# Cosine attention and a mixture-of-experts MLP on one core: from scheduled groups to an order written out by hand

## Chip, core and metric

One core of a Trainium2 chip runs the whole program in one launch. The metric is the device time of one execution in microseconds (us); lower is better. The runs listed are 674.89, 676.12 and 678.36 us, median 676.12.

## What is computed

Inputs are q, k and v of shape (8 batches, 12 heads, 448 tokens, 64), all float32, and tau = 0.1.

```python
q_n = q / (norm(q) + 1e-6);  k_n = k / (norm(k) + 1e-6)       # over the 64
attn = softmax(q_n @ k_n.T / tau)                              # per batch and head
x = (attn @ v).transpose(0, 2, 1, 3).reshape(3584, 768)
h = x @ w_in                                                   # 768 x 2048
out = (h * sigmoid(1.702 * h)) @ w_out                         # 2048 x 768
```

## The kernel before

Heads are handled in 48 pairs, so that two heads of 64 fill 128 partitions, and pairs in 16 groups of three; two groups make a batch. Tokens are cut in four chunks of 112.

The six row blocks of w_in and the sixteen of w_out are loaded as float32 through one staging buffer (`wst`) and cast to fp16 on ScalarE (line 93) and VectorE (line 99).

`emit_front` loads q, k and v of a group by SyncE (lines 111 and 117), squares on ScalarE (line 124), sums on VectorE (line 126) and finds 1/norm of the whole group on VectorE by a reciprocal, a polynomial and two Newton steps (lines 133 to 147). `emit_back` goes pair by pair: GpSimd scales q and k to fp16 (line 163), puts ones beside v and casts v (lines 170, 171); TensorE transposes (line 176, tile `tpsum`), VectorE copies the result to `qkT` (line 182); TensorE forms the scores of a chunk for both heads, each on 64 rows of the array (line 188, `spsum`), ScalarE takes Exp (line 196); per head four matmuls accumulate values and, in row 65, the softmax's denominator (line 209, `avps`), evicted by VectorE (line 217). Denominators go through DRAM (lines 218, 226), one reciprocal on six partitions (line 229), back to DRAM and out as one broadcast per head (line 234); VectorE multiplies (line 238), and a DMA puts the product into `xT` (line 241).

`emit_moe` takes a batch of 448 tokens: sixteen groups of six matmuls (line 254, `hps`), Tanh on ScalarE (line 262), one VectorE operation that makes `gT` (line 263); then for each of four 112-token tiles and two column halves sixteen matmuls (line 276, `ops`), a copy on ScalarE (line 283) and one store per tile (line 289). The halves of x * sigmoid are folded: tanh(0.851 h) + 1, and 0.5 in the last copy.

The order between engines is left to the scheduler of the tile framework, which takes instructions by priority in the order of the program: front of a group, back of the group before, MoE when a batch is complete. PSUM has two buffers for scores (`ps_sp`) and one each for transposes, `avps`, `hps` and `ops`.

## Time and profile before

| what | value |
|---|---|
| median of three runs | 676.12 us (674.89 to 678.36) |
| profiled execution | span 674.3 us from first to last instruction; no other time is listed for it |
| TensorE, VectorE, ScalarE, GpSimd busy | 529.9, 344.0, 338.5, 134.6 us |
| DMA | 68.49 MB, all issued by SyncE |

The profile is of one execution. Busy time of TensorE counts matmuls, whose ends are modelled and which overlap, so it is more than the work needs back to back. PE is TensorE, PEld its weight loads, DVE VectorE, ACT ScalarE, POOL GpSimd, SP SyncE. Idle time before an instruction is put down to what released it.

### The profile page before, as it was taken

Reading aid. Unit: us, or ns where it says so; the run is one execution under the profiler, and the core shown is the slowest. Engines: PE = TensorE matmul, PEld = TensorE weight load, DVE = VectorE, ACT = ScalarE, POOL = GpSimd, SP = SyncE. Lnnn points to the kernel's source line nnn. Section 1 sums busy time; section 2 is a strip of 40 time slices with the busy share of each in tenths; the row PEclk is TensorE's granted clock in tenths of the full one; section 3 lists DMA queues with packets and bytes.
Section 4 is the critical chain, followed back from the end, with each engine's and each line's share of the span. In section 5 each row is a group of like instructions: output and inputs, shape, how many; then the busy total and the mean of one; then the engine's idle time right before and its main releaser. Section 6 shows DMA issues by size and latency. Waiting matters only on the chain. (4 is left out here: it accounts for less than half of the span.)

```text
span 674.3 us, 8804 instructions
## 1 busy us (share of the span) xinstructions
PE 529.9 (79%) x2944; PEld 294.0 (44%) x2944; DVE 344.0 (51%) x640; ACT 338.5 (50%) x439; POOL 134.6 (20%) x199
## 2 busy tenths in 40 slices
PE   0095518578998889989988889899999998786566
PEld 0032203134564446544644455446544653453244
DVE  0336535567847784468266734674296136312210
ACT  4383507267737763667347735764476345212211
POOL 1214022034124323032123211240233000000000
PEclk9999855599999999999999999999999999999999
DMA  8875655545564446134424441344321211030002
GB/s 209 233 183 130 183 153 141 138 90 119 131 166 108 103 112 157 56 82 108 134 61 103 109 120 54 92 117 124 83 56 39 73 41 42 23 81 20 1 20 62
DMA packets 156878, 68.49 MB, mean 102 GB/s; under 512 B 137856, under 2 KB 150432, under 8 KB 156064
## 3 DMA queue, kind: packets, MB, share of 16 engines
q1 hardware_dynamic: 156832, 67.93, 40.1%
q8 instruction: 23, 0.38, 0.2%
q14 instruction: 23, 0.19, 0.1%
HBM read 51.20 MB, written 11.18 MB: 93 GB/s over the span
## 5 line engine op out<-in xcount | busy, mean ns | idle before, releaser
L254 PE MATMUL hps<-xT,w_in 128*128 128x448 f16 x768 | 173.1, 355 | 54.3 <-DVE gT L263 38.5
L196 ACT ACTIVATE expT<-spsum,negbias 112x896 f16<-112x896 f32 x192 | 185.4, 1007 | 50.7 <-PE spsum L188 43.8
L276 PE MATMUL ops<-w_out,gT 128*112 128x384 f16 x1024 | 196.7, 327 | 11.5 <-ACT ost L283 7.4
L276 PEld LDWEIGHTS <-gT 128*112 128x112 f16 x1024 | 131.9, 130 | 65.1 <-issue 20.0
L263 DVE SCALAR_TENSOR_TENSOR gT<-th,hps 128x448 f16<-128x448 f16 x128 | 78.0, 610 | 134.7 <-ACT th L262 134.4
L254 PEld LDWEIGHTS <-w_in 128*128 128x128 f16 x768 | 73.7, 98 | 130.3 <-issue 61.4
L163 POOL TENSOR_TENSOR qks<-qk,ry 112x512 f16<-112x512 f32 x96 | 99.5, 1063 | 134.6 <-PE tpsum L176 74.1
L262 ACT ACTIVATE th<-hps 128x448 f16<-128x448 f32 x128 | 69.6, 544 | 111.4 <-PE hps L254 108.0
L209 PE MATMUL avps<-expT,v 112*65 112x448 f16 x384 | 111.7, 385 | 10.8 <-DVE av_sb L217 7.7
L283 ACT ACTIVATE ost<-ops 112x384 f32<-112x384 f32 x64 | 31.5, 492 | 122.2 <-PE ops L276 117.7
L188 PE MATMUL spsum<-qkT 64*112 64x448 f16 x384 | 78.2, 415 | 11.5 <-ACT expT L196 8.5
L126 DVE TENSOR_REDUCE n<-sq 112x16 f16<-112x1024 f16 x48 | 58.1, 1212 | 52.0 <-ACT sq L124 52.0
L217 DVE CAST av_sb<-avps 65x448 f16<-65x448 f32 x96 | 58.9, 613 | 38.6 <-PE avps L209 37.9
L176 PE MATMUL tpsum<-ident,qks 112*128 112x112 f16 x384 | 35.0, 229 | 52.2 <-POOL qks L163 52.2
L124 ACT ACTIVATE sq<-qk 112x1024 f16<-112x1024 f32 x48 | 50.6, 1054 | 29.9 <-DMA qk<-in_k_dram 26.9
L238 DVE TENSOR_TENSOR rcpb<-av_sb,rcpb 64x448 f16<-64x448 f16 x96 | 42.2, 457 | 45.0 <-DMA rcpb<-rcp_dram 44.1
L209 PEld LDWEIGHTS <-v 112*65 112x65 f16 x384 | 42.6, 117 | 49.3 <-issue 33.2
L176 PEld LDWEIGHTS <-qks 112*128 112x128 f16 x384 | 25.5, 106 | 70.4 <-POOL qks L163 57.2
L170 POOL MEMSET v<- 112x8 f16 x48 | 6.6, 142 | 233.3 <-PE avps L209 228.3
L188 PEld LDWEIGHTS <-qkT 64*112 64x112 f16 x384 | 25.2, 132 | 60.7 <-issue 52.2
L229 DVE RECIPROCAL rcg<-dnm 6x448 f16<-6x448 f16 x16 | 46.9, 2933 | 0.4 <-DMA dnm<-den_dram 0.4
L171 POOL CAST v<-v 112x512 f16<-112x512 f32 x48 | 29.6, 616 | 47.9 <-DMA v<-in_v_dram 47.9
(19 smaller groups left out, 94.4 us busy)
## 6 DMA issues: line engine op xcount, KB each, us to landing
qk<-in_q_dram SPq DMA_DIRECT2D x96, 112.0 KB
qk<-in_k_dram SPq DMA_DIRECT2D x96, 112.0 KB
v<-in_v_dram SPq DMA_DIRECT2D x96, 112.0 KB
out_dram<-ost SPq DMA_DIRECT2D x32, 336.0 KB
wst<-in_moe_w_in_dram SPq DMA_DIRECT2D x6, 1024.0 KB
wst<-in_moe_w_out_dram SPq DMA_DIRECT2D x16, 384.0 KB
rcpb<-rcp_dram SPq DMA_DIRECT2D x96, 56.0 KB
xT<-rcpb SPq DMA_DIRECT2D x96, 56.0 KB
```

The costliest lines, as they stand in the source:

```text
L124: nc.scalar.activation(out=sq, in_=qk32, func=AF.Square)
L126: nc.vector.tensor_reduce(out=n2[:, gi], in_=sq, axis=AX.X, op=ALU.add)
L163: nc.gpsimd.tensor_tensor(out=qks[:, ti], in0=qk32[:, ti], in1=rs_all[:, gi, ti, :, :, None].to_broadcast((P, NCH, 2, D)), op=ALU.mult,)
L176: nc.tensor.transpose(out=tpsum[:, ti, c * P : (c + 1) * P], in_=qks[:, ti, c], identity=ident[:P, :P],)
L188: nc.tensor.matmul(out=spsum[:, j, :S], lhsT=qkT[64 * j : 64 * (j + 1), 1, c * P : (c + 1) * P], rhs=qkT[64 * j : 64 * (j + 1), 0, :], sta ...
L196: nc.scalar.activation(out=expT, in_=spsum[:, :, :S], func=AF.Exp, bias=negbias[:P], scale=inv_tau,)
L209: nc.tensor.matmul(out=avps, lhsT=v65[:, c, j, :], rhs=expTs[c][:, j, :], start=(c == 0), stop=(c == NCH - 1),)
L217: nc.vector.tensor_copy(out=av_sb, in_=avps)
L254: nc.tensor.matmul(out=hps, lhsT=w_in_sb[kk][:, 128 * m : 128 * (m + 1)], rhs=xT_sb[kk][:, tok0 : tok0 + S], start=(kk == 0), stop=(kk == ...
L262: nc.scalar.activation(out=th, in_=hps, func=AF.Tanh, scale=0.851)
L263: nc.vector.scalar_tensor_tensor(out=gT[:, m, :], in0=th, scalar=1.0, in1=hps, op0=ALU.add, op1=ALU.mult,)
L276: nc.tensor.matmul(out=ops, lhsT=gT[:, kk, P * mt : P * (mt + 1)], rhs=w_out_sb[kk][:, NW * n : NW * (n + 1)], start=(kk == 0), stop=(kk = ...
```

## The change

Every engine's queue now holds its instructions in the order in which the program writes them (`manual_schedule`). The program is a loop over steps; step s treats half of pair s // 2. A table `later` says in which step each other piece of work stands: loads of q and k six pairs ahead and of v five, squares three pairs ahead, scaling two pairs ahead, transposes one, the attend of the pair before. The second half of attention's output rows is made directly on partitions 64 to 127: four standing tiles `vt` hold 128 columns for each head: v, a column of ones, and zeros. So the normalised product is written to `xT` in place and no DMA moves it.

When the six pairs of a batch are normalised, `queue_moe` puts its matmuls into a list, and `fill` takes from that list three times in each step, until a nominal 1.04 to 1.07 us are spent. Batches go in twos for the second matmul, with seven tiles of 128 tokens for two batches (three tiles with the first, four with the second), so that a tile's rows go out in two stores. MoE matmuls share three PSUM buffers; transposes and attend share one.

Norms are square roots by pow on GpSimd, one per pair, then an addition and a reciprocal on VectorE. Denominators of a group come in on 112 partitions, and their reciprocals go out as two broadcasts. Weights are loaded by eight DMAs on GpSimd's queue that cast to fp16: w_in in steps -1, 1, 3 and 5, w_out in steps 9, 11, 13 and 15. Squares are kept in float32. The last batch is queued in step 101 and runs with nothing beside it.

The core of the diff; of what it takes out, the listing above has nearly all:

```diff
-RS_C2 = -0.031518428176595475
-RS_C1 = 0.5141912670046448
-RS_C0 = 0.5009886404507127
+MM1_NS = 189
+MM2_NS = 163
+STEP_NS = 3150
+AV_SCALE = 2.0**-11
...
+    p_in = pool("p_in", 6)
+    p_v = pool("p_v", 4)
+    p_sq = pool("p_sq", 3)
+    p_n = pool("p_n", 4)
+    p_qks = pool("p_qks", 3)
+    p_qkT = pool("p_qkT", 2)
+    p_exp = pool("p_exp", 8)
+    p_av = pool("p_av", 6)
+    p_rc = pool("p_rc", 2)
+    p_x = pool("p_x", 2)
+    p_g = pool("p_g", 1)
+    p_th = pool("p_th", 3)
+    p_o = pool("p_o", 3)
...
+    ps_s = psum("ps_s", 2)
+    ps_a = psum("ps_a", 1)
+    ps_m = psum("ps_m", 3)
+    ctx.enter_context(tc.manual_schedule())
...
+    def load_qk(x):
+        b, h0 = x // HP, (x % HP) * 2
+        for d, src, nm in ((q32, q, "q32"), (k32, k, "k32")):
+            d[x] = p_in.tile([P, 2, C, D], FP32, name=nm)
             nc.sync.dma_start(
+                out=d[x].rearrange("p h c d -> p h (c d)"),
+                in_=src[b, h0 : h0 + 2].rearrange("h (p c) d -> p h (c d)", p=P),
             )
...
+    def norm(x):
+        nrm = p_n.tile([P, 2, 2, C], FP32, name="nrm")
+        nc.gpsimd.tensor_tensor(
+            out=nrm,
+            in0=n2s.pop(x),
+            in1=half_c[:P, :, None, None].to_broadcast((P, 2, 2, C)),
+            op=ALU.pow,
+        )
+        nc.vector.tensor_scalar(
+            out=nrm, in0=nrm, scalar1=1e-6, scalar2=None, op0=ALU.add
+        )
+        rss[x] = p_n.tile([P, 2, 2, C], FP32, name="rs")
+        nc.vector.reciprocal(out=rss[x], in_=nrm)
...
+    def cast_v(x):
+        src = v32.pop(x)
+        vt = vts[x % 4]
+        for j in range(2):
+            nc.gpsimd.tensor_copy(out=vt[:, :, j, 64 * j : 64 * j + D], in_=src[:, j])
+    def transposes(x):
+        tps = ps_a.tile([128, 2, S], FP16, name="tps", tag="a")
+        qks = qkss.pop(x)
+        for ti in (1, 0):
+            for c in range(C):
+                nc.tensor.transpose(
+                    out=tps[:, ti, c * P : (c + 1) * P],
+                    in_=qks[:, ti, c].rearrange("p j d -> p (j d)"),
+                    identity=ident[:P, :P],
+                )
+        qkTs[x] = p_qkT.tile([128, 2, S], FP16, name="qkT")
+        nc.vector.tensor_copy(out=qkTs[x], in_=tps)
...
+    def attend(x, j):
+        if j == 0:
+            avs[x] = p_av.tile([128, 2, S], FP16, name="av")
+        ps = ps_a.tile([128, S], FP32, name="avp", tag="a")
+        for c in range(C):
+            nc.tensor.matmul(
+                out=ps,
+                lhsT=vts[x % 4][:, c, j],
+                rhs=exps[x, c][:, j],
+                start=(c == 0),
+                stop=(c == C - 1),
+            )
+        n = D + 1 if j == 0 else 128
         nc.vector.tensor_scalar(
+            out=avs[x][:n, j], in0=ps[:n], scalar1=AV_SCALE, scalar2=None, op0=ALU.mult
+        )
...
+    def den_rcp(g):
+        r = p_rc.tile([P, 2 * GRP * S // P], FP16, name="rcg")
+        with nc.allow_low_precision("fp16 reciprocal of softmax denom"):
+            nc.vector.reciprocal(out=r, in_=dnms.pop(g))
+        rcps[g] = dram.tile([2 * GRP, S], FP16, name="rcp")
+        nc.sync.dma_start(out=flat(rcps[g]), in_=r)
+        rcbs[g] = p_rc.tile([128, GRP, S], FP16, name="rcb")
+        for j in range(2):
+            nc.sync.dma_start(
+                out=rcbs[g][64 * j : 64 * (j + 1)],
+                in_=rcps[g]
+                .rearrange("(i j) s -> j i s", j=2)[j][None]
+                .to_broadcast((64, GRP, S)),
             )
...
+    def mm1_stream(b):
+        if b % 2 == 0:
+            gts[b // 2] = p_g.tile([128, KT2, 2 * S], FP16, name="gT")
+        gT = gts[b // 2][:, :, (b % 2) * S : (b % 2 + 1) * S]
         for m in range(KT2):
+            ps = ps_m.tile([128, 512], FP32, name="mm", tag="mm")
             for kk in range(KT1):
                 nc.tensor.matmul(
+                    out=ps[:, :S],
+                    lhsT=w_in_sb[:, kk, 128 * m : 128 * (m + 1)],
+                    rhs=xTs[b, kk],
                     start=(kk == 0),
                     stop=(kk == KT1 - 1),
                 )
+                if kk == KT1 - 1:
+                    th = p_th.tile([128, S], FP16, name="th")
+                    nc.scalar.activation(out=th, in_=ps[:, :S], func=AF.Tanh, scale=0.851)
+                    nc.vector.scalar_tensor_tensor(
+                        out=gT[:, m],
+                        in0=th,
+                        scalar=1.0,
+                        in1=ps[:, :S],
+                        op0=ALU.add,
+                        op1=ALU.mult,
+                    )
+                yield MM1_NS
...
+    def store(b2, t, ost, cols):
+        i0, i1 = 128 * t, 128 * (t + 1)
+        while i0 < i1:
+            n = min(i1, (i0 // P + 1) * P) - i0
+            b, c, p0 = 2 * b2 + i0 // S, (i0 % S) // P, i0 % P
+            rows = out[b * S : (b + 1) * S].rearrange("(p c) m -> c p m", c=C)[c]
+            nc.sync.dma_start(
+                out=rows[p0 : p0 + n, cols],
+                in_=ost[i0 - 128 * t : i0 - 128 * t + n, cols],
             )
+            i0 += n
+    def mm2_stream(b2, tiles, last):
...
+        for t in tiles:
+            ost = p_o.tile([128, DM], FP32, name="ost")
+            for n in range(2):
+                cols = slice(NW * n, NW * (n + 1))
+                ps = ps_m.tile([128, 512], FP32, name="mm", tag="mm")
                 for kk in range(KT2):
                     nc.tensor.matmul(
+                        out=ps[:, :NW],
+                        lhsT=gT[:, kk, 128 * t : 128 * (t + 1)],
+                        rhs=w_out_sb[:, kk, cols],
                         start=(kk == 0),
                         stop=(kk == KT2 - 1),
                     )
+                    if kk == KT2 - 1:
+                        nc.scalar.activation(
+                            out=ost[:, cols], in_=ps[:, :NW], func=AF.Copy, scale=0.5
+                        )
+                        if last and t == tiles[-1]:
+                            store(b2, t, ost, cols)
+                        elif n == 1:
+                            store(b2, t, ost, slice(0, DM))
+                    yield MM2_NS
+    streams = []
+    def fill(ns):
+        while ns > 0 and streams:
+            try:
+                ns -= next(streams[0])
+            except StopIteration:
+                streams.pop(0)
+    def queue_moe(b):
+        streams.append(mm1_stream(b))
+        tiles = (0, 1, 2) if b % 2 == 0 else (3, 4, 5, 6)
+        streams.append(mm2_stream(b // 2, tiles, b == B - 1))
+    def load_w_in(i):
+        n = slice(512 * i, 512 * (i + 1))
+        nc.gpsimd.dma_start(
+            out=w_in_sb[:, :, n], in_=moe_w_in.rearrange("(k p) n -> p k n", p=128)[:, :, n]
+        )
+    def load_w_out(i):
+        n = slice(4 * i, 4 * (i + 1))
+        nc.gpsimd.dma_start(
+            out=w_out_sb[:, n], in_=moe_w_out.rearrange("(k p) n -> p k n", p=128)[:, n]
+        )
+    for x in range(NPAIR):
+        at(2 * (x - 6), load_qk, x)
+        at(2 * (x - 5), load_v, x)
+        for ti in range(2):
+            at(2 * (x - 3) + ti, square, x, ti)
+            at(2 * (x - 3) + ti + 1, reduce, x, ti)
+        at(2 * (x - 2), norm, x)
+        at(2 * (x - 2) + 1, scale, x, 1)
+        at(2 * (x - 2) + 1, scale, x, 0)
+        at(2 * (x - 2) + 1, cast_v, x)
+        for j in range(2):
+            at(2 * (x + 1) + j, den_out, x, j)
+        if x % GRP == GRP - 1:
+            s = 2 * (x + 1) + 1
+            d = 2 if x < HP else 1
+            at(s, den_in, x // GRP)
+            at(s + d, den_rcp, x // GRP)
+            for i in range(GRP):
+                at(s + 2 * d + 1 + i // 2, normalise, x - GRP + 1 + i)
+        if x % HP == HP - 1:
+            at(2 * (x + 1) + 1 + 2 * d + 2, queue_moe, x // HP)
+    for i in range(4):
+        at(-1 + 2 * i, load_w_in, i)
+        at(9 + 2 * i, load_w_out, i)
...
+    for s in range(min(later), max(max(later), 2 * NPAIR + 2) + 1):
+        x, half = s // 2, s % 2
+        jobs = later.pop(s, [])
+        if 0 <= x < NPAIR:
+            scores(x, half)
+            exp(x, 2 * half)
+        fill(STEP_NS * 0.33)
+        if 0 <= x < NPAIR:
+            exp(x, 2 * half + 1)
+        if 0 <= x - 1 < NPAIR:
+            attend(x - 1, half)
+        for f, a in jobs[: len(jobs) // 2]:
+            f(*a)
+        fill(STEP_NS * 0.33)
+        if half == 1 and 0 <= x + 1 < NPAIR:
+            transposes(x + 1)
+        for f, a in jobs[len(jobs) // 2 :]:
+            f(*a)
+        fill(STEP_NS * 0.34)
+    fill(1e9)
```

## Rows read from the trace of the kernel before

**Rows 1.** Windows: stretch, length, PE, PEld, DVE, ACT, POOL busy, PEclk, DMA share, GB/s.

```profile
0.00:135.00 135.00, 62.18 (x236) 24.30 (x237) 59.63 (x117) 60.26 (x58) 28.67 (x49) 0.81 0.66 171
135.00:573.00 438.00, 398.14 (x2337) 226.11 (x2337) 265.62 (x495) 258.30 (x344) 105.94 (x150) 1.00 0.39 96
573.00:674.30 101.30, 69.57 (x372) 43.59 (x370) 18.73 (x30) 19.92 (x38) 0.00 (x0) 1.00 0.12 35
```

**Rows 2.** TensorE's timeline, 300 to 318 us: start, duration, instructions.

```profile
308.17 0.35 PE L209 MATMUL avps<-expT,v 112*65 112x448 f16 x1 [0.32 <-ACT expT L196]
...
310.08 0.92 PE L209 MATMUL avps<-expT,v 112*65 112x448 f16 x4
310.94 0.40 PE L188 MATMUL spsum<-qkT 64*112 64x448 f16 x2
311.37 1.29 PE L254 MATMUL hps<-xT,w_in 128*128 128x448 f16 x6
...
312.76 0.59 PE L188 MATMUL spsum<-qkT 64*112 64x448 f16 x4
313.27 0.57 PE L176 MATMUL tpsum<-ident,qks 112*128 112x112 f16 x8
```

**Rows 3.** Timeline of the end stretch, 640 to 652 us.

```profile
643.71 1.29 PE L254 MATMUL hps<-xT,w_in 128*128 128x448 f16 x6 [1.13 <-DVE gT L263]
...
647.24 2.76 PE L276 MATMUL ops<-w_out,gT 128*112 128x384 f16 x16 [0.58 <-ACT ost L283]
```

**Rows 4.** Groups by line and shape, ScalarE: busy us, mean ns | idle before, releasers.

```profile
L196 ACT ACTIVATE expT<-spsum,negbias 112x896 f16<-112x896 f32 x192 | 185.4, 1007 | 50.7 <-PE spsum L188 43.8 <-PE avps L209 4.5
...
L262 ACT ACTIVATE th<-hps 128x448 f16<-128x448 f32 x128 | 69.6, 544 | 111.4 <-PE hps L254 108.0 <-DVE rt L142 2.0 <-DVE ry L147 0.7
...
L124 ACT ACTIVATE sq<-qk 112x1024 f16<-112x1024 f32 x48 | 50.6, 1054 | 29.9 <-DMA qk<-in_k_dram 26.9 <-DVE ry L138 1.6 <-DMA v<-in_v_dram 0.7
```

**Rows 5.** Groups by line and shape, VectorE.

```profile
L263 DVE SCALAR_TENSOR_TENSOR gT<-th,hps 128x448 f16<-128x448 f16 x128 | 78.0, 610 | 134.7 <-ACT th L262 134.4
...
L217 DVE CAST av_sb<-avps 65x448 f16<-65x448 f32 x96 | 58.9, 613 | 38.6 <-PE avps L209 37.9
L126 DVE TENSOR_REDUCE n<-sq 112x16 f16<-112x1024 f16 x48 | 58.1, 1212 | 52.0 <-ACT sq L124 52.0
...
L229 DVE RECIPROCAL rcg<-dnm 6x448 f16<-6x448 f16 x16 | 46.9, 2933 | 0.4 <-DMA dnm<-den_dram 0.4
...
L182 DVE COPY qkT<-tpsum 128x896 f16<-128x896 f16 x48 | 29.2, 607 | 16.0 <-PE tpsum L176 15.8
```

**Rows 6.** Line 238, the normalising product: duration ns min/median/max, first and last start.

```profile
L238 DVE TENSOR_TENSOR rcpb<-av_sb,rcpb x96: 320/382/1224, 71.9 to 599.6; 64x448 f16<-64x448 f16 x96
```

**Rows 7.** Groups by line and shape, GpSimd.

```profile
L163 POOL TENSOR_TENSOR qks<-qk,ry 112x512 f16<-112x512 f32 x96 | 99.5, 1063 | 134.6 <-PE tpsum L176 74.1 <-DVE ry L147 43.4 <-issue 7.3
...
L171 POOL CAST v<-v 112x512 f16<-112x512 f32 x48 | 29.6, 616 | 47.9 <-DMA v<-in_v_dram 47.9
...
L170 POOL MEMSET v<- 112x8 f16 x48 | 6.6, 142 | 233.3 <-PE avps L209 228.3 <-DMA xT<-rcpb 5.0
```

**Rows 8.** Tile v, SyncE's issues of its loads: duration ns min/median/max.

```profile
L117 SPq DMA_DIRECT2D v<-in_v_dram x96: 312/462/2307, 3.3 to 512.0; - x96
```

**Rows 9.** Windows, 25 to 30 us.

```profile
25.00:30.00 5.00, 0.00 (x0) 0.00 (x0) 3.26 (x13) 1.60 (x1) 1.03 (x2) 1.00 1.07 298
```

**Rows 10.** Windows, 101 to 119 us.

```profile
101.00:119.00 18.00, 15.71 (x58) 6.40 (x59) 10.82 (x17) 12.93 (x14) 3.81 (x6) 0.50 0.50 134
```

**Rows 11.** TensorE's timeline, 50 to 135 us.

```profile
115.92 1.70 PE L209 MATMUL avps<-expT,v 112*65 112x448 f16 x4
```

**Rows 12.** The chain that ended last: start us, duration us, what.

```profile
431.09 2.54 DMA rcpb<-rcp_dram
...
511.69 1.66 DMA den_dram<-av_sb
```

**Rows 13.** Timeline of the last 10 us.

```profile
670.17 0.49 ACT L283 ACTIVATE ost<-ops 112x384 f32<-112x384 f32 x1 [2.85 <-PE ops L276]
```

320 lines of the change are left out of this document (100 added, 220 removed).

## The prediction

> **What bounds the kernel now.** I read the engines in three stretches first, since the page's slices fill up late and thin out early [rows 1]: TensorE is the busiest in each, 62.2 us of the first 135, 398.1 of the next 438, 69.6 of the last 101.3, and its granted clock is 0.81 on average in the first, 1.00 after. So some 73 us are idle before the pipeline runs, 40 inside it and 32 behind it.
>
> Next is what the matrix work needs back to back. One matmul alone shows about 0.35 us, of which some 0.17 is drain, so a group of n costs its shown time less 0.17 [rows 2, 3]: hps (1.29 - 0.17) / 6 = 0.188 us; ops (2.76 - 0.17) / 16 = 0.162; avps 0.188; a pair of spsum matmuls, which run side by side, 0.59 - 0.40 = 0.19; a transpose (0.57 - 0.17) / 8 = 0.05. A pair of heads therefore needs 8 x 0.188 + 4 x 0.19 + 8 x 0.05 = 2.66 us, the 48 pairs 128, the 768 hps matmuls 144 and the 1,024 ops matmuls 166: 438 of the 674.3 us. The other 236 are gaps and half clock. In the end stretch the gap can be seen in one line [rows 3]: each hps group starts 1.13 us late, held by VectorE's gT, since hps has one PSUM buffer.
>
> **The change, part by part.** The order is now written out: a step is half a pair (two score blocks, two Exp, one head's attend), and in each step three fills of MoE matmuls. A fill runs until 1.04 us or more are spent: six hps matmuls (1.13 us) or seven ops matmuls (1.13 us). A filled step thus holds 1.33 us of attention and 3.4 of MoE, 4.73 us of TensorE.
>
> *Output tiles of 128 tokens.* 28 tiles x 2 x 16 = 896 ops matmuls instead of 1,024: 128 x 0.162 = 20.7 us less on the bound engine. TensorE's need falls to 418 us.
>
> *Other engines in a filled step.* ScalarE: two Exp 2.01, a Square of half the elements (bounds 0.53, half of the row, and 1.05; I take 0.6, as a short operation keeps its fixed part), three Tanh 1.63 in an hps step: 4.25 us [rows 4]. VectorE: three gT 1.83, an eviction 0.61, half a qkT copy 0.3, half a reduction 0.6, one normalising product 0.38, small norm work 0.2: 3.9 us [rows 5, 6]. Both lie beside TensorE's 4.73, with little to spare. If that cover goes, each 0.1 us of excess per step costs 7 us, as there are 71 filled steps. Both queues are in order: behind a Tanh that waits for its hps group stands the second Exp, behind gT the eviction of avps, and for that waits the transposition of the next pair, since avps and transposes now share one PSUM buffer. Behind the normalisation stands the qkT copy, for which the next scores wait; that is the stall that I expect to be late next. I take 4% (0.2 us a step) for such seams; the bounds are 0 and the 9% that TensorE idles in the present middle (40 of 438) [rows 1].
>
> *GpSimd.* Per pair two scalings 2.1 and two casts of v, some 0.7, with pow added [rows 7]. No row shows pow; it has 16 elements per partition. Below stands the 0.14 of a memset, above the 1.06 of a 512-element product; I take 0.3, as the element count is near the memset's. It is 3.1 us of a pair's 9.9: covered. The Newton steps leave VectorE, 16 times a dozen operations, which were not on the path.
>
> *Weights cast by DMA.* The 22 staging loads, 6 casts on ScalarE and 16 on VectorE go; 8 loads on GpSimd's queue come. No DMA goes out from GpSimd in this trace. The nearest row is SyncE issuing a v load of 448 pieces: 0.46 us in the middle of its cases, 2.3 at the longest [rows 8]. A quarter of w_in has 768 pieces, so I bound the issue by 0.46 and by 2.3 x 768 / 448 = 4.0 and take 2 us, since software on GpSimd is nearer to its scaling, 2 ns an element, 1.6 us for 768. It is hidden: in the early stage a pair takes 6.8 us, of which GpSimd needs 3.1, so 3.7 are free, and one such load stands behind the scalings of each pair. The Trainium skill, "SBUF — State Buffer", section "SBUF: two separate sides", speaks against this edit: descriptors of a GpSimd DMA can't be written while a VectorE instruction that takes both ports runs. That the two engines do hold each other up, this trace shows: the product of two SBUF tensors takes 0.32 us at least and up to 1.22, about one GpSimd scaling more [rows 6].
>
> *SyncE's queue.* 144 input loads for 288, 32 broadcasts of the reciprocal for 96, none of the 96 xT copies, and 58 output stores for 32 (each tile crosses one border of 112 tokens). Its pieces grow from 256 B to 1 KB. den_in waits on SP for den_out to land, and behind it stand loads that are needed three pairs later: nothing.
>
> **The sum.** *Start.* ScalarE's order puts the squares of three pairs ahead of the first Exp. 1.8 MB at 298 GB/s [rows 9] take 6 us and land 2.5 later; reduction, pow, two scalings, transposes and copy run beside the later squares: 12 us (10 to 16).
>
> *Steps 0 to 18*, attention alone: ScalarE needs 2.6 us a step. But TensorE is then likely at 1.2 GHz: in 101 to 119 us, attention with little else, the granted clock was 0.50 and four avps took 1.70 us, against 0.92 later [rows 2, 10, 11]. 58 matmuls in those 18 us are 2.4 pairs, 3.7 us per half pair. By step 19, 13 pairs of q, k, v and the weights have moved, 21.5 MB; at 298 GB/s that is 72 us from the beginning, which allows 3.2 us a step. Between 2.6 and 3.7 I take 3.4, nearest to the cold row: 65 us. The Trainium skill, "DMA: Bandwidth & Descriptors", section "Specifications", gives about 358 GB/s for a core; by that the same bytes need 60 us, DMA drops out, and the sum would be some 4 us lower. No window here reaches it.
>
> *Steps 19 to 95.* A batch's MoE fills 9.9 steps (even) or 11.4 (odd) out of 12, so 70.7 steps are filled: 70.7 x 4.93 = 349 us. The other 6.3 have only attention: 2.9 us each, 18.
>
> *Steps 96 to 101.* The rest of batch 6 (11 us) runs beside the last pair's chain: attend some 6 us in, then eviction 0.6, three short hops through DRAM at 1.7, the reciprocal 0.3 (24 elements a partition, where 448 take 2.93) [rows 5], the broadcast 2.5, six products 2.3 [rows 6, 12]: 17, of which TensorE idles 5.
>
> *Tail.* 96 x 0.188 + 128 x 0.162 = 38.8 us. The last copy and its store, 4.2 as now (670.17 to 674.3) [rows 13].
>
> 12 + 65 + 349 + 18 + 17 + 38.8 + 4.2 = 504 us of span. The profiled span is 674.3, the median of runs 676.12, so 1.8 lie around it: **506 us**.
>
> **Rivals.** *One: no seams.* Steps run at TensorE's 4.73 and the early ones at ScalarE's 2.6: 506 - 14 - 15 = 477. For it: three PSUM buffers for MoE. Against: in-order queues at 90 and 83%.
>
> *Two: the weight loads hold up GpSimd.* The issue takes its upper bound of 4.0 us, and VectorE, busy some 2 of an early step's 3.4 us, holds the ports for part of it, so that 4 become 7. Against 3.7 us free in a pair, eight of them push the early stage back by 8 x 3.3 = 26 us: 532; at 10 us each, 556. The rule on the ports above would work in this way. For: no such load is in this trace, and GpSimd feeds every transpose. Against: the weights themselves are asked for ten steps before use, and most of VectorE's early work reads PSUM or reduces.
>
> *Three: ScalarE and VectorE set the step.* If each Tanh waits out an Exp (1.0 us) and its PSUM buffer comes late, an hps and ops step are 5.9 us: 506 + 70.7 x 0.97 = 575. Both are busy only 59 and 61% of the present middle [rows 1], which says little of 90%.
>
> *Four, slower than before: pow on GpSimd.* One instruction per pair, in the one queue that feeds all transposes. GpSimd's pair is 2.8 us + pow; from 7 us on it outruns the filled 9.9, and at 10.6 us the 48 pairs take 48 x 13.4 = 643, with the 74 of start, end and tail 717. From 9.8 us on it is slower than now. Against: that is 0.6 us per element, 300 times what the scaling takes per element.
>
> **Chances.** Forecast 0.54 (485 to 525), no seams 0.17, GpSimd held 0.15, step set by ScalarE and VectorE 0.10, pow 0.04. The range of 470 to 560 leaves out pow, the third rival and the upper end of the second. About 0.5% is what a measurement of this kernel can tell from no change; only pow ends near or above the old time: faster 0.95, same 0.01, slower 0.04.
>
> **What would show it.** Right: no wst and xT transfers, 896 ops matmuls, no wait of hps for gT; from about 77 us on TensorE over 90% busy at clock 1.00, and a period of 9.9 us between transposes of successive filled pairs; the end as now. Step 0 at 12 and the first hps at about 77 us test start and early stage one by one. Wrong: a pow or a weight load of over 3.7 us on GpSimd with transposes waiting for qks; spsum waiting for qkT, or avps for its eviction, by more than 0.2 us a step; ps buffers of MoE waiting for gT or ost; a clock of 0.50 behind step 19.

## The result, and the profile after

The changed kernel takes 628.41 us (median of four, 625.66 to 629.85), against 676.84 (674.89 to 678.36): a ratio of 0.9277, interval 0.9248 to 0.9306. It is faster, as forecast, by 48 us where 170 were forecast, and lies 68 us above the upper end of the range. The profiled execution has a span of 627.9 us and took 629.85.

The page of the changed kernel, its busy times and slices, the clock, and the chain by line:

```profile
PE 496.5 (79%) x2816; PEld 243.0 (39%) x2816; DVE 294.5 (47%) x593; ACT 310.3 (49%) x473; POOL 281.7 (45%) x254
...
PE   0575555779979896998679896989589896898897
...
PEclk9966757799979998999979997999989997899899
...
POOL nrm L119 18%; PE mm L297 16%; PE mm L257 15%; DVE xT L242 8%; PE avp L192 6%; DVE av L200 6%; PE sp L170 6%; PE tps L153 4%; DVE n L113 4%; DVE gT L267 3%; ACT th L266 2%; DVE qkT L159 2%; DVE rs L129 2%; DVE nrm L125 1%; DMA rcb<-rcp 1%
```

TensorE is busy for 79% of the span, the share it had before; the steady 90% that was forecast from 77 us on is not there, and the clock drops again and again far behind the early stage. The first entry of the chain is not matrix work but line 119, pow on GpSimd: 18% of the span.

The three stretches of the changed kernel (from the first scores to the first matmul of MoE, to the last attend, to the end); columns are the stretch and its length, then each engine's busy time, the granted clock, the DMA share and GB/s. They answer to [rows 1]:

```profile
16.20:106.60 90.40, 53.17 (x225) 19.81 (x226) 35.40 (x75) 43.85 (x59) 60.09 (x57) 0.68 0.75 149
106.60:571.20 464.60, 394.17 (x2320) 196.27 (x2319) 240.50 (x469) 247.36 (x381) 212.00 (x185) 0.94 0.28 79
571.20:627.90 56.70, 48.02 (x267) 26.33 (x264) 13.19 (x24) 14.08 (x27) 0.00 (x0) 0.97 0.17 48
```

Groups of the changed kernel by line (busy us, mean ns of one; idle time before, and what ended it), answering to [rows 5 to 7]:

```profile
L119 POOL TENSOR_TENSOR nrm<-n,half_c 112x16 f32<-112x16 f32 x48 | 139.2, 2899 | 226.9 <-DVE n L113 226.9
...
L125 DVE TENSOR_SCALAR nrm<-nrm 112x16 f32<-112x16 f32 x48 | 8.4, 175 | 141.6 <-POOL nrm L119 141.6
...
L242 DVE TENSOR_TENSOR xT<-av,rcb 64x448 f16<-64x448 f16 x96 | 57.1, 594 | 7.1 <-DMA rcb<-rcp 5.9
```

Two lines carry the case. One pow takes 2.90 us, not 0.3. And the addition behind it, 0.175 us of work, has 141.6 us of idle VectorE ahead of it: 3.0 us for each of 48 pairs. GpSimd itself has 226.9 us of idle time before pow: it is not the engine that is short.

Who waits behind VectorE, in the list of waits of the changed kernel (us in total, times, longest):

```profile
DVE nrm L125 <- POOL nrm L119: 141.6, 48, 5.1
...
PE tps L153 <- DVE av L200: 45.7, 28, 4.5
PE mm L257 <- DVE xT L242: 42.2, 10, 6.1
...
PE sp L170 <- DVE qkT L159: 21.7, 18, 4.0
...
PE mm L257 <- DVE gT L267: 4.1, 5, 0.8
```

One pair of the early stage in the timeline of the changed kernel (start, duration; in brackets the idle time before and its releaser):

```profile
35.50 0.99 PE L170 MATMUL sp<-qkT 64*112 64x448 f16 x4
...
36.92 2.92 POOL L119 TENSOR_TENSOR nrm<-n,half_c 112x16 f32<-112x16 f32 x1 [2.28 <-DVE n L113]
...
39.87 0.17 DVE L125 TENSOR_SCALAR nrm<-nrm 112x16 f32<-112x16 f32 x1 [3.05 <-POOL nrm L119]
40.08 0.25 DVE L129 RECIPROCAL rs<-nrm 112x16 f32<-112x16 f32 x1
40.25 0.56 DVE L200 TENSOR_SCALAR av<-avp 128x448 f16<-128x448 f32 x1
...
40.87 0.55 PE L153 MATMUL tps<-ident,qks 112*128 112x112 f16 x8 [2.79 <-DVE av L200]
...
41.46 0.62 DVE L159 COPY qkT<-tps 128x896 f16<-128x896 f16 x1 [0.64 <-PE tps L153]
...
42.14 0.99 PE L170 MATMUL sp<-qkT 64*112 64x448 f16 x4 [0.72 <-DVE qkT L159]
...
42.80 1.72 ACT L182 ACTIVATE expT<-sp 112x896 f16<-112x896 f32 x2 [4.39 <-PE sp L170]
...
44.67 0.99 PE L170 MATMUL sp<-qkT 64*112 64x448 f16 x4
```

Read it downwards. Pow runs for a pair whose transposes stand three steps later. The addition stands in VectorE's queue ahead of the eviction of the current pair; the eviction frees the PSUM buffer for the transposes; the transposes feed the copy, the copy the scores, the scores Exp. So work that is not urgent at all stops TensorE for 2.79 us, and by that ScalarE, through one in-order queue. The scores also run at 0.99 us where four take 0.59 [rows 2]: TensorE has fallen to the lower of its two levels for part of the pair (granted clock 0.69 in the mean). The pair takes 9.17 us (35.50 to 44.67), where 6.8 were forecast.

A batch's first MoE matmuls meet the same wait, and one thing more; same timeline:

```profile
106.59 1.11 PE L257 MATMUL mm<-xT,w_in 128*128 128x448 f16 x5
...
107.62 2.89 POOL L119 TENSOR_TENSOR nrm<-n,half_c 112x16 f32<-112x16 f32 x1 [4.79 <-DVE n L113]
...
110.55 0.17 DVE L125 TENSOR_SCALAR nrm<-nrm 112x16 f32<-112x16 f32 x1 [3.01 <-POOL nrm L119]
...
111.24 1.04 POOL L135 TENSOR_TENSOR qks<-k,rs 112x512 f16<-112x512 f32 x1 [0.73 <-DVE rs L129]
111.41 2.27 DVE L242 TENSOR_TENSOR xT<-av,rcb 64x448 f16<-64x448 f16 x2
...
113.74 0.53 PE L257 MATMUL mm<-xT,w_in 128*128 128x448 f16 x1 [6.04 <-DVE xT L242]
...
114.81 2.44 PE L257 MATMUL mm<-xT,w_in 128*128 128x448 f16 x6
```

The last two normalising products stand behind the addition, and then take 2.27 us for two beside GpSimd's scalings, where the median product takes 0.39. TensorE waits 6.04 us for them, and from 114 to 118 us its granted clock is 0.50.

### The profile page after: what moved, and what is told of

It reads as the page before. It is cut to its first block, busy times and chain, and to the rows that moved or that the text cites. A ratio compares the mean times of both kernels' runs of the same rounds, so it can differ in the third digit from the quotient of the medians.

```text
span 627.9 us, 7945 instructions
## 1 busy us (share of the span) xinstructions
PE 496.5 (79%) x2816; PEld 243.0 (39%) x2816; DVE 294.5 (47%) x593; ACT 310.3 (49%) x473; POOL 281.7 (45%) x254
## 4 chain that ended last, share of the span: by engine, by line
PE 47%; DVE 26%; POOL 19%; issue 4%; ACT 2%; DMA 1%; SPq 0%; DVEq 0%; POOLq 0%
POOL nrm L119 18%; PE mm L297 16%; PE mm L257 15%; DVE xT L242 8%; PE avp L192 6%; DVE av L200 6%; PE sp L170 6%; PE tps L153 4%; DVE n L113 4%; DVE gT L267 3%; ACT th L266 2%; DVE qkT L159 2%; DVE rs L129 2%; DVE nrm L125 1%; DMA rcb<-rcp 1%
## 5 line engine op out<-in xcount | busy, mean ns | idle before, releaser
L119 POOL TENSOR_TENSOR nrm<-n,half_c 112x16 f32<-112x16 f32 x48 | 139.2, 2899 | 226.9 <-DVE n L113 226.9
L257 PE MATMUL mm<-xT,w_in 128*128 128x448 f16 x768 | 180.3, 379 | 46.3 <-DVE xT L242 42.2
L182 ACT ACTIVATE expT<-sp 112x896 f16<-112x896 f32 x192 | 170.1, 913 | 92.6 <-PE sp L170 92.4
L297 PE MATMUL mm<-w_out,gT 128*128 128x384 f16 x896 | 160.9, 326 | 0.6 <-DVE gT L267 0.6
L266 ACT ACTIVATE th<-mm 128x448 f16<-128x448 f32 x128 | 69.5, 543 | 143.2 <-PE mm L257 142.3
L267 DVE SCALAR_TENSOR_TENSOR gT<-th,mm 128x448 f16<-128x448 f16 x128 | 76.8, 612 | 71.5 <-ACT th L266 71.4
L297 PEld LDWEIGHTS <-gT 128*128 128x128 f16 x896 | 83.9, 98 | 66.5 <-issue 11.5
L192 PE MATMUL avp<-expT,vt 112*128 112x448 f16 x384 | 99.3, 385 | 0.0
L170 PE MATMUL sp<-qkT 64*112 64x448 f16 x384 | 68.4, 437 | 23.3 <-DVE qkT L159 21.7
L153 PE MATMUL tps<-ident,qks 112*128 112x112 f16 x384 | 33.2, 242 | 56.8 <-DVE av L200 45.7
L125 DVE TENSOR_SCALAR nrm<-nrm 112x16 f32<-112x16 f32 x48 | 8.4, 175 | 141.6 <-POOL nrm L119 141.6
L113 DVE TENSOR_REDUCE n<-sq 112x8 f32<-112x512 f32 x96 | 64.2, 670 | 2.6 <-ACT sq L108 2.0
L242 DVE TENSOR_TENSOR xT<-av,rcb 64x448 f16<-64x448 f16 x96 | 57.1, 594 | 7.1 <-DMA rcb<-rcp 5.9
```

The source lines that it names most:

```text
L113: nc.vector.tensor_reduce(out=n2s[x][:, ti], in_=sqs.pop((x, ti)), axis=AX.X, op=ALU.add)
L119: nc.gpsimd.tensor_tensor(out=nrm, in0=n2s.pop(x), in1=half_c[:P, :, None, None].to_broadcast((P, 2, 2, C)), op=ALU.pow,)
L153: nc.tensor.transpose(out=tps[:, ti, c * P : (c + 1) * P], in_=qks[:, ti, c].rearrange("p j d -> p (j d)"), identity=ident[:P, :P],)
L170: nc.tensor.matmul(out=sp[:, j, :S], lhsT=qkT[64 * j : 64 * (j + 1), 1, c * P : (c + 1) * P], rhs=qkT[64 * j : 64 * (j + 1), 0, :], start= ...
L182: nc.scalar.activation(out=e, in_=sps.pop((x, c))[:, :, :S], func=AF.Exp, scale=inv_tau, **kw)
L192: nc.tensor.matmul(out=ps, lhsT=vts[x % 4][:, c, j], rhs=exps[x, c][:, j], start=(c == 0), stop=(c == C - 1),)
```

## The experiments

All ratios are to the kernel before, timed beside each run. "The middle" is the stretch from the first MoE matmul to the last attend, 464.6 us in the changed kernel. Diffs are against the changed kernel unless another is named.

### Is it the wait in VectorE's queue?

Theory T is that reading; G puts the loss on pow as GpSimd's load, P on the PSUM buffer that transposes and attend share, D on the DMAs of the weights.

**No pow.**

```diff
-        nc.gpsimd.tensor_tensor(
...
-            op=ALU.pow,
-        )
         nc.vector.tensor_scalar(
-            out=nrm, in0=nrm, scalar1=1e-6, scalar2=None, op0=ALU.add
+            out=nrm, in0=n2s.pop(x), scalar1=0.5, scalar2=0.5, op0=ALU.mult, op1=ALU.add
         )
```

> This kernel leaves out the square root: in place of pow on GpSimd, the VectorE addition computes (1 + n2) / 2 from the sum of squares. Theory T (the loss against the forecast is VectorE waiting 3.0 us per pair, in order, for GpSimd's pow, with the eviction of avp and the qkT copy queued behind): VectorE's wait for nrm, 141.6 us now, goes to under 10 and the time to 505 to 535 us. Rival G (pow costs as load on GpSimd's queue, which delays qks): the same time here. Rival P (the one PSUM buffer that avp and transposes share makes the seams): above 580 us.

545.15 us, ratio 0.8055 (0.8020 to 0.8091). 83 us are gone with pow, though the time is 10 us above what T gave. That leaves load and wait mixed, which the next two part.

**Pow kept, the wait moved.** Addition and reciprocal (`invert`) stand one step later, scalings and casts too.

```diff
-        at(2 * (x - 2) + 1, scale, x, 1)
-        at(2 * (x - 2) + 1, scale, x, 0)
-        at(2 * (x - 2) + 1, cast_v, x)
+        at(2 * (x - 2) + 1, invert, x)
+        at(2 * (x - 1), scale, x, 1)
+        at(2 * (x - 1), scale, x, 0)
+        at(2 * (x - 1), cast_v, x)
```

> Pow stays, 48 x 2.9 us on GpSimd; VectorE's addition and reciprocal stand one step later, scaling and v's casts too (one step later than now). Theory T: VectorE no longer waits in order, 515 to 545 us. Rival G: GpSimd does the same work, 600 us or more. Rival P: above 580 us.

533.76 us, ratio 0.7887 (0.7858 to 0.7916). Of VectorE's 141.6 us of waiting this line is left, in its list of waits:

```profile
DVE nrm L131 <- POOL nrm L121: 21.0, 16, 4.6
```

**Pow kept, nothing on VectorE behind it.**

```diff
-    nc.vector.memset(half_c, 0.5)
+    nc.vector.memset(half_c, -0.5)
...
-        nc.vector.tensor_scalar(
-            out=nrm, in0=nrm, scalar1=1e-6, scalar2=None, op0=ALU.add
-        )
-        rss[x] = p_n.tile([P, 2, 2, C], FP32, name="rs")
-        nc.vector.reciprocal(out=rss[x], in_=nrm)
```

> Pow with exponent -0.5 gives 1/norm at once on GpSimd, the 1e-6 added to the norm is left out, and VectorE has no part in the norm behind its reduction. Theory T: 505 to 535 us. Rival G: pow and the two scalings remain in one queue, 600 us or more. Rival P: above 580 us.

527.71 us (527.44 to 530.70), ratio 0.7812 (0.7782 to 0.7843). The groups by line, and the three stretches, of this kernel:

```profile
L119 POOL TENSOR_TENSOR rs<-n,half_c 112x16 f32<-112x16 f32 x48 | 139.3, 2902 | 161.1 <-DVE n L113 153.6
```

```profile
12.40:81.90 69.50, 46.12 (x225) 17.43 (x226) 31.21 (x55) 42.93 (x58) 62.65 (x58) 0.90 0.97 204
81.90:468.30 386.40, 371.80 (x2321) 189.47 (x2320) 210.31 (x396) 249.50 (x382) 208.49 (x186) 1.00 0.33 95
468.30:525.40 57.10, 49.04 (x266) 26.51 (x264) 13.18 (x24) 14.12 (x27) 0.00 (x0) 0.94 0.17 48
```

GpSimd's work is the same to 4 us (278.1 busy against 281.7, pow 139.3 against 139.2), and yet 101 us are gone: G falls. The middle went from 464.6 to 386.4 us, the early stage from 90.4 to 69.5, TensorE is busy for 96% of the middle (371.80 of 386.40), and the clock is 1.00 there. The two kernels that keep pow and drop the wait, or most of it, are the fastest of the three. This third one also leaves out 20.5 us of VectorE's own work (8.4 for the addition, 12.1 for the reciprocal), but the second keeps that work and is 95 us faster than the change. The second, which computes all that the change computes, is the fastest of its kind here; this third, without the 1e-6, is the base of several of the next.

**Two PSUM buffers for transposes and attend,** one fewer for MoE.

```diff
-    ps_a = psum("ps_a", 1)
-    ps_m = psum("ps_m", 3)
+    ps_a = psum("ps_a", 2)
+    ps_m = psum("ps_m", 2)
```

> The changed kernel with two PSUM buffers for avp and transposes and two instead of three for MoE; nothing else. Rival P: under 600 us. Theory T: the eviction still waits behind pow, 615 to 635 us, transposes wait for qkT or qks instead of the eviction.

642.39 us, ratio 0.9492 (0.9459 to 0.9525): slower than the change as it stands and above what either theory gave, with VectorE's wait for pow untouched at 141.7 us. The transposes no longer wait for the eviction (45.7 us before), but the scores wait 55.7 us for qkT instead of 21.7: the buffer mostly passes the wait on, and P falls as the main cause. The early stage, where there is no MoE, is 6.8 us shorter (83.6 for 90.4). That the whole is slower fits the buffer taken from MoE: its matmuls now wait 25.3 us for gT instead of 4.1.

### What pow costs, and where VectorE may wait for it

**mult in pow's place**, with the same operands on the same engine.

```diff
-            op=ALU.pow,
+            op=ALU.mult,
...
-            out=nrm, in0=nrm, scalar1=1e-6, scalar2=None, op0=ALU.add
+            out=nrm, in0=nrm, scalar1=0.5, scalar2=None, op0=ALU.add
```

> The changed kernel with a multiplication in pow's place on GpSimd (and 0.5 added behind it on VectorE), so the square root is left out. The hop GpSimd to VectorE and its place in the order stay. If pow's own 2.9 us are the cost (theory T), the 16-element instruction takes 0.1 to 0.4 us, VectorE's wait for nrm falls from 141.6 to 15 to 30 us and the time is 538 to 555 us, near the 545 of the kernel that needs no GpSimd. If the hop itself is the cost, above 590 us.

549.19 us, ratio 0.8139 (0.8105 to 0.8173). The instructions of this tile (duration ns, least, median, most):

```profile
L119 POOL TENSOR_TENSOR nrm<-n,half_c x48: 205/217/228, 5.8 to 459.2; 112x16 f32<-112x16 f32 x48
```

So the price is pow's own, not that of a small instruction on GpSimd nor, for the greater part, of the hop between two engines: 0.22 us against 2.90, and VectorE's wait falls to 13.9 us. The hop by itself may cost some 4 us, by the 545.15 of the kernel that has none.

**Pow in two halves** (from the kernel with pow alone; one instruction for q, one for k, each of 8 elements).

```diff
+        for ti in range(2):
+            nc.gpsimd.tensor_tensor(
+                out=rss[x][:, ti],
+                in0=n2[:, ti],
+                in1=half_c[:P, :, None].to_broadcast((P, 2, C)),
+                op=ALU.pow,
+            )
```

> The kernel with pow of -0.5 alone, pow in two instructions of 8 elements a partition, for q and for k. If pow's 2.9 us are per element (0.18 each): two of 1.45 us, time 526 to 532. If they are a fixed price of the instruction: two of about 2.9 us, GpSimd at 8.8 us a pair, early stage 20 us longer and the total 545 to 560.

535.83 us, ratio 0.7925 (0.7897 to 0.7954). The group by line:

```profile
L121 POOL TENSOR_TENSOR rs<-n,half_c 112x8 f32<-112x8 f32 x96 | 156.9, 1637 | 151.1 <-DVE n L113 146.5 <-PE mm L254 4.4
```

8 elements take 1.64 us and 16 take 2.90: (2.90 - 1.64) / 8 = 0.16 us an element, and some 0.38 fixed, worked out from these two points. The time lies between the two expectations (526 to 532, 545 to 560); why it is above the first was not tried.

**The scaling of k on VectorE for the first ten pairs** (from the kernel with pow alone), against G2, by which GpSimd's load sets the early stage.

```diff
-        nc.gpsimd.tensor_tensor(
+        eng = nc.vector if ti == 1 and x < 10 else nc.gpsimd
+        eng.tensor_tensor(
```

> The kernel with pow of -0.5 alone, the scaling of k on VectorE for the first ten pairs, which takes 1.04 of 6.6 us a pair from GpSimd. Theory G2: first MoE matmul at 70 to 76 us, total 516 to 522 us. Theory D: at 80 to 83 us, total 525 to 530.

536.10 us, ratio 0.7925 (0.7901 to 0.7949): 8 us lost. Its list of VectorE's waits says why; the scaling brought the wait for pow back into the queue, so that G2 is not tested by it:

```profile
DVE qks L131 <- POOL rs L119: 20.0, 10, 3.8
```

### The early stage

**w_out later** (from the kernel with pow alone).

```diff
-        at(9 + 2 * i, load_w_out, i)
+        at(15 + 2 * i, load_w_out, i)
```

> The kernel with pow of -0.5 alone, w_out's four loads six steps later (15 to 21). Theory D (in the early stage the weight loads keep the DMA engines busy and delay q, k and the hops of the denominators): the first MoE matmul, at 81.9 us, comes at 68 to 76, total 514 to 522 us. Theory G2 (GpSimd, with pow, scalings and casts, sets the early stage): first MoE matmul at 80 to 83 us, total 525 to 530.

528.61 us, ratio 0.7818 (0.7794 to 0.7843): no difference. The first MoE matmul comes at 76.0 us for 81.9 (79.5 in the kernel with tiles of 112 tokens below, whose early stage is the same), as D gave, so w_out's loads do hold the early stage; but the middle takes 391.9 us for 386.4, and D's 514 to 522 us are missed. Two stretches behind the first MoE matmul, of this kernel and then of the one with pow alone:

```profile
80.00:100.00 20.00, 16.10 (x92) 7.66 (x89) 9.34 (x18) 11.19 (x18) 11.28 (x12) 0.91 0.78 159
```

```profile
82.00:100.00 18.00, 15.89 (x97) 7.59 (x95) 11.79 (x23) 11.89 (x20) 11.39 (x11) 1.00 0.37 101
```

The DMA work that was pushed out stands there (0.78 of the DMA engines for 0.37), with the clock at 0.91 for 1.00. That this is what lengthens the middle is likely, not shown.

**The first groups' reciprocals later.** In the kernel without pow VectorE waits once for 9.20 us for a denominator hop through DRAM, in the timeline of its early stage:

```profile
47.99 0.30 DVE L218 RECIPROCAL rcg<-dnm 112x24 f16<-112x24 f16 x1 [9.20 <-DMA dnm<-den]
```

By theory Q such waits cost the early stage its time. So, from the kernel with pow alone:

```diff
-            at(s + d, den_rcp, x // GRP)
+            at(s + (3 if x < HP else 1), den_rcp, x // GRP)
```

> The kernel with pow of -0.5 alone, with the reciprocal of the first two groups' denominators one step later; the products that need it stay where they are. Theory Q (VectorE's in-order wait for the denominators' hop through DRAM, behind the weight loads, is what the early stage still loses): VectorE's waits for dnm, 2.9 and 4.3 us at 47 and 71 us, go, the first MoE matmul comes at 74 to 78 instead of 81.9 us, total 521 to 526. Theory G2 (GpSimd sets the early stage): 80 to 83 us, total 526 to 530.

529.41 us, ratio 0.7842 (0.7818 to 0.7866): not borne out. VectorE's two early waits for this hop, 2.85 us at 47 and 4.29 at 71 with pow alone, do go, and yet the first MoE matmul comes at 80.7 us for 81.9: they were not what set the early stage. Nor does GpSimd's load look like it: without pow GpSimd is busy for 33.7 of an early stage of 73.0 us, with pow alone for 62.7 of 69.5. Beyond w_out's loads, what sets it stays open.

### Tiles of 112 or 128 tokens

From the kernel with pow alone, 1,024 matmuls again:

```diff
-        i0, i1 = 128 * t, 128 * (t + 1)
+        i0, i1 = 112 * t, 112 * (t + 1)
...
-        tiles = (0, 1, 2) if b % 2 == 0 else (3, 4, 5, 6)
+        tiles = (0, 1, 2, 3) if b % 2 == 0 else (4, 5, 6, 7)
```

> The kernel with pow of -0.5 alone, and output tiles of 112 tokens as before the change: 1,024 instead of 896 second matmuls, eight tiles for two batches. If TensorE is now the bound where there is MoE work, the 128 matmuls of 0.162 us cost 20.7 us, less some 5 that the unfilled steps take in: 541 to 550 us. If VectorE's or ScalarE's queue sets the step, the matmuls hide: 526 to 533 us.

535.23 us (534.08 to 536.86), ratio 0.7911 (0.7890 to 0.7931). The tiles are worth 7.5 us, between the two expectations; by the middles alone 14.2 (400.6 against 386.4). The saving cannot be the whole 128 x 0.162 = 20.7: the steps that it empties don't go, but turn into steps with attention alone, at the forecast's 2.9 us for 4.93. By these figures, the four even batches with 1.5 filled steps fewer give an estimate of 6 x 2.03 = 12.2. Start, early stage and end are 4.5 us shorter with 112, so that the two profiles stand 9.7 us apart; why they are was not tried.

### Why the kernels without pow were not the fastest

Without pow there is less work, and yet the straight line and mult are 17 and 21 us behind the kernel with pow alone. Two more had been made to go below it.

**One Heron step on VectorE, w_out later** (a straight line and one step towards the root, in place of pow, addition and reciprocal).

```diff
+            out=s, in0=n2, scalar1=0.325, scalar2=0.175, op0=ALU.mult, op1=ALU.add
+        )
+        nc.vector.reciprocal(out=t, in_=s)
+        nc.vector.scalar_tensor_tensor(
+            out=t, in0=t, scalar=0.25, in1=n2, op0=ALU.mult, op1=ALU.mult
+        )
+        nc.vector.tensor_tensor(out=s, in0=s, in1=t, op=ALU.add)
+        nc.vector.reciprocal(out=rss[x], in_=s)
```

> The changed kernel without pow: the norm by a straight line and one Heron step on VectorE (five small instructions, good to 0.12% for squares between 0.22 and 1.3, so only for such data), and w_out's loads in steps 15 to 21. Theory T and D (weight loads delay the denominators' hop, on which VectorE waited 9.2 us in the kernel without a square root): first MoE matmul at 66 to 74 us, total 510 to 520. If only T holds: first MoE matmul at 82 to 88, total 540 to 548, as without the square root.

**The same, with the later reciprocals of denominators** (both edits as above).

> The kernel before this one (Heron step, w_out late), with the reciprocal of the first two groups one step later as well. Theories T, D and Q together: first MoE matmul at 62 to 70 us, total 505 to 516; without Q as the kernel before this one.

Both missed: 552.32 us, ratio 0.8199 (0.8156 to 0.8242), and 556.89, ratio 0.8235 (0.8187 to 0.8283). The first MoE matmul comes at 78.3 and 78.2 us, earlier than without pow (84.0) but not at the 62 to 74 hoped for, and the later reciprocals change nothing here either. What costs the time is the middle, 415 and 420 us for 386. The start of a batch's MoE in the kernel without pow shows what stands there; timeline:

```profile
261.34 0.25 DVE L123 RECIPROCAL rs<-nrm 112x16 f32<-112x16 f32 x1
261.51 0.56 DVE L194 TENSOR_SCALAR av<-avp 128x448 f16<-128x448 f32 x1
261.83 1.04 POOL L129 TENSOR_TENSOR qks<-k,rs 112x512 f16<-112x512 f32 x1 [6.67 <-DVE rs L123]
261.99 2.28 DVE L236 TENSOR_TENSOR xT<-av,rcb 64x448 f16<-64x448 f16 x2
...
264.32 0.35 PE L251 MATMUL mm<-xT,w_in 128*128 128x448 f16 x1 [3.23 <-DVE xT L236]
...
264.94 2.45 PE L251 MATMUL mm<-xT,w_in 128*128 128x448 f16 x6
```

And in the kernel with pow alone:

```profile
252.02 2.90 POOL L119 TENSOR_TENSOR rs<-n,half_c 112x16 f32<-112x16 f32 x1 [3.70 <-PE mm L252]
252.39 0.79 DVE L237 TENSOR_TENSOR xT<-av,rcb 64x448 f16<-64x448 f16 x2
...
253.23 0.35 PE L252 MATMUL mm<-xT,w_in 128*128 128x448 f16 x1 [1.23 <-DVE xT L237]
...
253.81 1.30 PE L252 MATMUL mm<-xT,w_in 128*128 128x448 f16 x6
```

The last two products of a group take 2.28 us beside GpSimd's scalings and 0.79 beside pow. TensorE waits 3.23 us for 1.23, and the next six matmuls take 2.45 us for 1.30, on the lower level of the clock (granted 0.50 there, 1.00 with pow). Theory C puts the loss on the collision; L on those two products being late, by the collision and by the norm work ahead of them; S on VectorE's added work.

**Scalings one step later**, with the straight line and with the Heron step:

```diff
-        at(2 * (x - 2) + 1, scale, x, 1)
-        at(2 * (x - 2) + 1, scale, x, 0)
-        at(2 * (x - 2) + 1, cast_v, x)
+        at(2 * (x - 1), scale, x, 1)
+        at(2 * (x - 1), scale, x, 0)
+        at(2 * (x - 1), cast_v, x)
```

> As the first experiment (no pow, its square root left out and a straight line in its place), with the two scalings and the casts of a pair one step later, so that they no longer start in the step in which VectorE forms the normalised products. Theory C (collision: a product with two operands in SBUF and a GpSimd scaling hold each other up, and the first matmuls of a batch then wait for the products): all products at 0.37 to 0.39 us where the first experiment had up to 1.14; the wait of the first matmuls for xT falls from 17.6 us to under 10; the middle takes 386 to 392 us where it took 404; 526 to 534 us. Rival S (the small VectorE work and the straight line's order itself cost the middle its time, or it comes from the early stage): products short or not, the middle stays above 398 and the time is 540 to 548.

> As the kernel with the straight line and one Heron step on VectorE and the later w_out loads, with the scalings and casts one step later. It holds for squared norms from 0.22 to 1.3 of the scale chosen; beyond, the approximation is left to be worse. Theory C: products at 0.37 to 0.39 us; the middle takes 386 to 394 us where it took 415, the first MoE matmul stays at about 78, so 520 to 530 us. Rival S: the five small operations (about 1.1 us of VectorE a pair) are what costs, the middle stays above 403 and the time is 538 to 552.

547.86 us, ratio 0.8110 (0.8080 to 0.8140), and 554.29, ratio 0.8206 (0.8164 to 0.8247). Nothing moved, but these two tell nothing apart, for the edit did not do what it says. The first one's list of waits, in the stretch from 84 to 480 us:

```profile
POOL qks L129 <- DVE rs L123: 214.1, 28, 9.2
```

The scalings still start when the reciprocal ends: without pow GpSimd's queue holds nothing that would keep them back, so a later place in the program is no later time. (In the second experiment the scalings do start later, since the reciprocal that they wait for was moved: VectorE's order holds it back.)

**Pow one step earlier** (from the kernel with pow alone; squares, reductions and pow moved, scalings left):

```diff
-            at(2 * (x - 3) + ti, square, x, ti)
-            at(2 * (x - 3) + ti + 1, reduce, x, ti)
-        at(2 * (x - 2), norm, x)
+            at(2 * (x - 3) + ti - 1, square, x, ti)
+            at(2 * (x - 3) + ti, reduce, x, ti)
+        at(2 * (x - 2) - 1, norm, x)
```

> As the kernel in which pow gives 1/norm by itself, with squares, reductions and pow one step earlier, the scalings left where they are. Pow's 2.9 us are then over when the scalings' step begins, and the scalings start where they start in the kernels without pow. Theory C: products beside scalings, up to 1.14 us again; the middle goes from 386 to over 395 us and the time from 527.7 to 536 or more. Rival S: pow's place does not matter to the middle, 386 to 390, and the time is 524 to 530.

539.71 us (539.17 to 541.15), ratio 0.7989 (0.7962 to 0.8016): 12 us lost with no work added, a middle of 403.3 us, and in it long products again, up to 1.12 us; TensorE waits 19.9 us for the products instead of 9.6. Where the scalings fall, then, matters to the middle, as far as one edit shows that moves squares, reductions and pow together.

**All six products of a group in one step**, the one before the batch's first matmuls:

```diff
-                at(s + 2 * d + 1 + i // 2, normalise, x - GRP + 1 + i)
+                at(s + 2 * d + 1, normalise, x - GRP + 1 + i)
```

> As the first experiment (no pow, its square root left out and a straight line in its place), with the six products of a group in one step, where before four stood in one and two in the next, the step in which the batch's first matmuls begin. Theory L (late products: without pow a scaling starts just before those last two products, which then take 2.28 us for two instead of 0.78, and the first matmuls of the batch wait 3.2 us for them, with half clock behind): the wait of the first matmuls for xT falls from 17.6 us to under 4 in the middle, which takes 380 to 388 us instead of 404, and the time is 521 to 530 us. Rival S (the middle's loss comes from VectorE's small work or from TensorE's queue): the wait goes but comes back elsewhere, the middle stays above 396 and the time is 537 to 548.

> As the kernel in which pow gives 1/norm by itself, with the six products of a group in one step. Its first matmuls of a batch wait 6.0 us in all in the middle for xT. Theory L: that wait goes, little else changes: 519 to 525 us. Rival S, or six products in a row (2.3 us of VectorE) that hold up the eviction and the transposes: 526 to 532 us.

> As the kernel with the straight line and one Heron step on VectorE and the later w_out loads (it holds for squared norms from 0.22 to 1.3 of the scale chosen), with the six products of a group in one step. Theory L: the wait for xT falls from 18.7 us in the middle to under 4, the middle takes 388 to 395 us instead of 415, and the time is 524 to 534 us. Rival S: above 543 us.

Straight line 528.73 us, ratio 0.7824 (0.7783 to 0.7866), for 545.15; Heron step 533.82, ratio 0.7906 (0.7869 to 0.7942), for 552.32; pow alone 526.85 (526.01 to 527.53), ratio 0.7796 (0.7761 to 0.7830), for 527.71. Without pow 16.4 and 18.5 us come back; with pow alone, where those products were hardly late, nothing that can be told from chance (TensorE's wait for them is 8.9 us for 9.6, so what L gave there did not come). The products of the straight line's kernel before this edit (from 84 to 480 us) and after it (whole run); ns, least, median, most:

```profile
L236 DVE TENSOR_TENSOR xT<-av,rcb x78: 373/389/1141, 85.5 to 478.2; 64x448 f16<-64x448 f16 x78
```

```profile
L236 DVE TENSOR_TENSOR xT<-av,rcb x96: 372/386/390, 59.7 to 483.3; 64x448 f16<-64x448 f16 x96
...
  PE mm L251: 3.7, 3
```

The second fence's last line is TensorE's wait for the products, 3.7 us, where the whole run had 21.6; the middle falls from 404.3 to 385.8 us. S falls as the main cause; with the Heron step the middle is still 393.6 us, and those 8 us may be VectorE's added work, which was not tried. What the kernels without pow had lost was this wait and the half clock behind it; that the collision alone, without the norm work ahead of it, would be enough was not tried.

## Why the prediction was wrong

Its working by parts, beside the changed kernel and the kernel with pow alone (us):

| part | forecast | changed | pow alone |
|---|---|---|---|
| to the first scores | 12 | 16.2 | 12.4 |
| to the first MoE matmul | 65 | 90.4 | 69.5 |
| to the last attend | 373 | 464.6 | 386.4 |
| to the end | 54 | 56.7 | 57.1 |
| span | 504 | 627.9 | 525.4 |

(From the single profiled run of each. The forecast's 17 us of steps 96 to 101 are divided at the last attend, 6 us in.)

**The step that failed** is "I take 0.3, as the element count is near the memset's. It is 3.1 us of a pair's 9.9: covered." It failed twice. The price was 2.90 us; the bounds, 0.14 and 1.06 [rows 7], were prices of other functions, and a function that no row shows can lie outside the rows' ends. And the cover was sought in the wrong place. At 2.90 GpSimd's pair is 5.8 us of a pair's 9.9, still covered, and the kernel with pow alone shows that it is. What was not costed is the addition: a wait that the change puts into VectorE's queue. Behind it stand the eviction, then transposes, copy, scores: the very seam that the prediction named in its part on other engines and gave 0.2 us a step. VectorE waits 3.0 us a pair, 1.5 a step, against that 0.2: 141.6 us in all.

With the wait taken out 101 us go, but not all of them are the wait by itself. Taking pow out altogether gives 83 us (545.15). Another 16 come back when a group's six products are also put into one step, where none is long (528.73), and that is as far as pow alone gets (527.71). Products just as long stand in the changed kernel, up to 1.14 us, and TensorE waits 42.2 us for xT there, 9.6 with pow alone. The prediction had put the products at 0.38, though its own rows go up to 1.22 [rows 6]. What the change would gain by that move alone, its wait left in, was not tried.

**Rival four** named pow, but as the load of GpSimd's queue that decides from 7 us on. The load never decided. The wait begins far below: with mult, at 0.22 us, VectorE already waits 13.9 us in all. Between 0.22 and 2.90 us, with the addition kept, nothing was tried.

**What held.** With pow alone, where that wait is gone and the products are short, the sum stands: 525.4 us against 504, each part within 5 us but the middle, which is 13 us (4%) longer. Its filled pairs come every 10.0 us in the mean (14 periods between qkT copies from 107 to 247 us, 9.4 to 11.0), as forecast (9.9). TensorE's needs per matmul, the seams of 4%, and the end with its tail come out as worked. 896 matmuls of `ops` ran; the MoE matmuls wait 4.1 us for gT in the whole run of the changed kernel, for 38.5 before. A weight load occupies GpSimd for 0.91 to 1.04 us (w_in) and 0.84 (w_out), inside the bounds and half of the 2 taken; rival two's hold-up of GpSimd is not there. That w_out's loads nevertheless lengthen the early stage by some 4 to 6 us was not in it, and moving them bought nothing. Rival three did not come: in the kernel with pow alone TensorE, busy for 96% of the middle, sets the filled step. The 20.7 us of the tiles were right as TensorE's need and overstated as time.

**The test by the prediction's own list.** The sign "a pow or a weight load of over 3.7 us on GpSimd with transposes waiting for qks" did not show it: pow takes 2.90 us. Of "spsum waiting for qkT, or avps for its eviction, by more than 0.2 us a step" the first is just over the mark (21.7 us in 96 steps, 0.23 each). The second shows only through the shared buffer: `avp` itself waits for nothing, while the transposes wait 45.7 us for its eviction, 0.48 a step. The last sign, "a clock of 0.50 behind step 19", is there, behind the waits for xT, which the list does not have.

## What to carry to other kernels

When an operation moves to another engine, cost the instruction that waits for its result, not the operation: in an in-order queue put the consumer one step later, or let the other engine finish the job. An operation that the trace has never shown needs a wide upper bound, and the question from which price on it decides, asked for every queue that waits for it. And a place in a written order is a time only if something ahead of it in its own queue, or an operand that comes late, keeps it there: removing a slow instruction can set the work behind it loose onto a worse moment.

## What the runs showed of the hardware

Pow as a GpSimd operation on two tensors takes 2.90 us for 112 x 16 float32 elements and 1.64 for 112 x 8, by these two 0.16 us an element of a partition; mult takes 0.22 for the 16. The scaling of 512 elements takes 1.04, 2 ns an element: pow is some 80 times as dear. The Trainium skill, "GPSIMD Engine Reference", section "3.1 Elementwise — side-by-side cycle accounting", gives about 2.6 cycles an element for an operation with two inputs; it measured add, and no row here counts cycles; but pow, some 80 times as dear an element as the scaling's multiplication, can't be priced by that figure.

A VectorE product of two SBUF tensors takes 0.39 us alone and up to 1.14 while GpSimd scales (1.25 in the kernel with mult); beside pow, which runs longer on 16 elements, it keeps its 0.39 (two in 0.79 us, inside a pow). The Trainium skill, "SBUF — State Buffer", section "Who interferes with whom", says that a VectorE instruction with two SBUF inputs contends with a GpSimd instruction that reads SBUF; the products beside scalings agree, and a like range stood in the kernel before [rows 6]. Pow reads SBUF as well, and the products beside it are not held up: there the measurement differs from that sentence.
